# Attention with decay and two MLPs: the softmax's reciprocal sums move from p to x, and p is split in two instructions per head

## The chip, the cores and the metric

The kernel runs on one core of a Trainium2 chip. The core has five engines that run side by side, each through its own list of instructions in order: TensorE (PE, matrix products; its weight loads are the rows PEld), VectorE (DVE), ScalarE (ACT), GpSimd (POOL) and SyncE (SP, which here issues the transfers). They wait for each other by semaphores. The metric is the time of one execution in microseconds, lower is better.

## The reference

```python
scores = q @ k.T / sqrt(64);  decay = cum[:, None] - cum[None, :]      # cum: running sum of log f
scores = where(causal, scores + decay, -1e9) - max
attn = exp(scores);  attn = attn / (sum(attn) + 1e-9)                  # per row (query)
x = (attn @ v)                 # 4 batches x 8 heads, 576 queries, head size 64
x = x.transpose(0, 2, 1, 3).reshape(2304, 512)
h = x @ w_in                   # 512 -> 2048
y = (max(h, 0) + alpha * min(h, 0)) @ w_out
out = ((y @ w_a) * (y @ w_b)) @ w_o          # 512 -> 1536 -> 512
```

## The kernel before

**Attention.** The 32 heads are worked in slots, `attention()`: slot u holds the softmax of head u, the transposition of p of head u-1 and the product of p with v of head u-2 (`lag` 2). What a slot does and in which order is written out as a list of short names, one list for even and one for odd slots: `T` makes the operands of the next head, `s0` to `s3` are scores and softmax of 128 query rows each, `R` those of the last 64 rows of two heads together (a row block `r` for a pair of heads), `ri` and `rr` the reciprocals of the row sums, `h0`..`h4` and `l0`..`l4` the handling of p, `p0` and `p1` the products with v for query columns 0 to 255 and 256 to 575, `M` a place where MLP work is let in. A scheduler of the framework then settles each engine's own order from this program.

**p in two ways.** Heads 0 to 9 ("native") keep p in f32: POOL multiplies each of the four row blocks by its reciprocal sum (`p_hi`, line 393), TensorE transposes it in 128x128 pieces (line 415), and DVE or ACT copy it out of PSUM. Heads 10 to 31 split p into two f16 parts: POOL writes the high part of p times the reciprocal (`p_hi`, line 406), DVE the rest (`p_lo`, line 486), four instructions of each per head, one per row block of 128, 256, 384 and 512 columns, and one of each per pair for `r` (640 columns). A transfer (DMA transpose, line 493) turns row blocks 0 and 1 together (`PT_lo`), 2 and 3 together (`PT_hi`) and `r` (`PT_r`). The f16 tiles `p16` have one buffer each, so the next head's high part waits for the transfer of the last.

**x.** `pv` leaves two halves in PSUM: ACT copies one (line 541), DVE adds the other (line 542). After the second head of a pair ACT rounds x to `xh` (line 204) and POOL subtracts to `xl` (line 548), once per half of the columns. x holds one pair of heads as 128 partitions (2 heads x 64) by 576 queries. Native heads do the same from one PSUM bank (lines 470, 471). After the last head of a batch both parts go to DRAM (line 557).

**Around it.** While the native heads run, 14 weight blocks of the first MLP are loaded and split by ACT, DVE and POOL (`weight`, lines 120 to 130). From slot 10 on, TensorE fills up with the first MLP (`mlp1a`; DVE line 636, POOL line 638), in a quota per slot. After the last slot the attention's buffers are closed, the rest of the first MLP, further weights (line 120 again) and the second MLP follow; there the instructions are the same before and after the change.

Of the kernel before, what the change touches and what calls it, by code (L numbers as in the profile page):

```python
# [35 lines left out]

REBIAS = 2.0 ** -112
_P = dict(
    even="ri T h3 h2 h0 s2 vs M h1 Q s0 M l2 s3 M s1 l1 M l0 l3 p0 p1 V po M W".split(),
    odd="ri h3 h2 h0 R rr vs h1 M Q l2 T l3 s2 M h4 s3 l1 M M s1 l0 s0 p0 p1 V W po l4 M".split(),  # L40
    split=0,
    lag=2,
    eng={'U': 'pool', 'xl': 'pool', 'h0': 'pool', 'h1': 'pool', 'nq': 'act', 'x': 'dve'},
    psm=3,
    first=10,
    rates=[0, 1, 1, 1, 0.8, 1.15, 1.15, 0.95],
# [5 lines left out]
    eng0={'h3': 'pool', 'U': 'pool', 'h1': 'pool', 'e0': 'act', 'e2': 'act', 'e3': 'dve', 'e4': 'dve'},
    even0=['ri', 's3', 'T', 'p0', 'h2', 'h3', 's2', 'vs', 'h1', 's0', 'Q', 'M', 'M', 'M', 'M', 'l1', 'l2', 'h0', 's1', 'l0', 'l3', 'p1', 'V', 'po', 'W', 'M'],
    odd0=['ri', 'h3', 'h2', 'h0', 'R', 'h1', 'rr', 'M', 'Q', 'l2', 'T', 'l3', 'M', 's3', 'h4', 's2', 'l1', 'l0', 'M', 'M', 's1', 's0', 'p0', 'vs', 'p1', 'V', 'W', 'po', 'l4', 'M'],
# [19 lines left out]
def decay_attention_then_two_mlps(ctx, tc, q, k, v, f, w_in, w_out, alpha, w_a, w_b, w_o, out):  # L74
# [135 lines left out]
    def attention_setup():  # L210
        a = lpool(right, "att1", 1, "right")
        ap_["a"] = a
        maskz = a.tile([128, ST + 128 + S - HB], BF16, name="maskz")
# [10 lines left out]
        ap_["mask_r"] = rest

        for i in range(2):
            z = ST + SR * (1 - i)
            t1 = a.tile([128, SP], F32R, tag=f"T1_{i}", name=f"T1_{i}")
            u1 = a.tile([128, S], F32R, tag=f"U1_{i}", name=f"U1_{i}")
            tu2 = a.tile([128, 2 * SP], F32R, tag=f"TU2_{i}", name=f"TU2_{i}")  # L230
            dve.memset(f32(t1)[:, z:z + SR], 0.0)
            dve.memset(f32(tu2)[0:68, z:z + SR], 0.0)
            TU[i] = t1, tu2[:, :SP], u1, tu2[:, SP:SP + S], f32(tu2)
            ap_["s", i] = a.tile([128, 1280], F32, tag=f"s_{i}", name=f"s_{i}")
            for nm in ("nm", "sm", "ri"):
# [244 lines left out]

    def p_lo(n, i):
        if n < NATIVE:
            return p_whole(n, i)
        t, s, ri = p16.pop((n, i))
        g, o = GROUP[i]
        eng(f"l{i}", "dve").scalar_tensor_tensor(t[:, 1::2, :], s, ri, t[:, 0::2, :], op0=ALU.mult, op1=ALU.subtract)
        whole, done_ = p16[n, g]
        done_.append(i)
        if g == "r" or len(done_) == 2:
            PT[n, g] = ap_["a2"].tile(  # L490
                [128, GSIZE[g], 128], F16, tag=f"PT_{g}", name=f"PT_{n}_{g}", bufs=2 if g == "r" else LAG,
            )
            sp.dma_start_transpose(out=PT[n, g], in_=whole.rearrange("p t n -> p (t n)"))
            del p16[n, g]

    def pv(u, c):

# [35 lines left out]
        x32 = xs[g, c]
        x = x32[p0:p0 + 64]
        if eng("x", "dve") is pool:
            y = ap_["a"].tile([128, 256 + SR], F32, tag="y", name=f"y_{u}_{c}")[p0:p0 + 64, :w]
            act.activation(x, ps_o[p0:p0 + 64, :w], AF.Copy, scale=1.0 / PSCALE)
            act.activation(y, ps_o[o0:o0 + 64, :w], AF.Copy, scale=1.0 / PSCALE)
            pool.tensor_tensor(x, x, y, op=ALU.add)
        else:  # L540
            act.activation(x, ps_o[o0:o0 + 64, :w], AF.Copy, scale=1.0 / PSCALE)
            dve.scalar_tensor_tensor(x, ps_o[p0:p0 + 64, :w], 1.0 / PSCALE, x, op0=ALU.mult, op1=ALU.add)
        if j == 0:
            return
        x_tiles(b)
        xh, xl = (x_[:, hp, h0:h0 + w] for x_ in X[b])
        dup(eng("xh", "act"), xh, x32)
        eng("xl", "pool").tensor_tensor(xl, x32, f32(xh), op=ALU.subtract)
# [364 lines left out]
```

## Time and profile before

| what | value |
|---|---|
| median of 3 runs | 1132.21 us (1131.31 to 1134.94) |
| profiled execution | 1132.38 us, span 1130.6 us, mean granted TensorE clock 0.988 |
| native heads with weights | about 20 to 118 us |
| split heads with the first MLP | about 118 to 380 us |
| rest of the first MLP with new weights | about 380 to 440 us |
| from there on TensorE is busy all the time, but for a stretch at 600 to 660 us | to the end |

The span runs from the first to the last instruction. Busy times of engines overlap; a matmul's row lasts longer than the distance to the next one's start, since they are pipelined.

### The profile page before, as it was taken

What the parts mean: (1) busy time and instruction counts of PE and PEld (TensorE: products, weight loads), DVE (VectorE), ACT (ScalarE), POOL (GpSimd) and SP (SyncE); (2) the same over time, 40 slices, a digit from 0 to 9 for tenths busy, and PEclk for the clock granted to TensorE, in tenths of its full rate; (3) what the DMA queues carried; (4) which work ended last, traced back from release to release, by engine and by line L of the source; (5) the groups of instructions that cost most, each with busy time, mean ns of one, the idle gap of its engine ahead of it and who ended that gap; (6) DMA issues with size and microseconds to landing.
All of it is one profiled execution on the core that took longest, in us unless ns stands there. A gap on an engine that the chain in (4) does not pass through costs nothing.

```text
span 1130.6 us, 18926 instructions
## 1 busy us (share of the span) xinstructions
PE 1074.1 (95%) x6663; PEld 1006.2 (89%) x6663; DVE 572.1 (51%) x1360; ACT 525.0 (46%) x1407; POOL 489.4 (43%) x627
## 2 busy tenths in 40 slices
PE   5989999999999988999998899999999999999998
PEld 3768988888888988999998899999999999999997
DVE  5787979888888386787777645200000000000001
ACT  5776776777677465555665544221121111211211
POOL 5554757667576354555566554211111111111111
PEclk9999999999999999999999999999999999999999
DMA  4646366776864774777788883020020200200000
GB/s 108 160 130 182 76 142 121 191 139 122 203 136 87 198 229 126 251 259 254 244 267 271 276 294 115 17 84 1 1 84 1 66 19 1 84 1 1 28 1 28
DMA packets 210772, 141.24 MB, mean 125 GB/s; under 512 B 138421, under 2 KB 196789, under 8 KB 210677
## 3 DMA queue, kind: packets, MB, share of 16 engines
q1 hardware_dynamic: 210676, 140.03, 44.4%
q8 instruction: 52, 0.85, 0.3%
q14 instruction: 44, 0.35, 0.1%
HBM read 88.30 MB, written 33.65 MB: 108 GB/s over the span
## 4 chain that ended last, share of the span: by engine, by line
PE 62%; DVE 16%; DMA 7%; ACT 6%; issue 4%; POOL 4%; SPq 1%; POOLq 0%; ACTq 0%; DVEq 0%
PE a L643 4%; PE a L641 4%; PE a L642 4%; PE b L643 4%; PE b L641 4%; PE b L642 4%; PE o L641 4%; PE o L643 4%; PE o L642 4%; PE hb L641 3%; PE hb L642 3%; PE hb L643 3%; PE ya L641 3%; PE ya L642 3%; PE ya L643 3%
## 5 line engine op out<-in xcount | busy, mean ns | idle before, releaser
L876 DVE TENSOR_TENSOR as<-b,as 128x384 f32<-128x384 f32 x72 | 40.2, 558 | 380.0 <-PE b L643 379.2
L878 POOL TENSOR_TENSOR gg<-as,gg 128x384 fp32r<-128x384 f32 x72 | 73.1, 1016 | 346.3 <-ACT gg L877 346.3
L875 ACT COPY as<-a 128x384 f32<-128x384 f32 x72 | 34.6, 481 | 182.7 <-PE a L643 182.7
L877 ACT CAST gg<-as 128x384 fp32r<-128x384 f32 x72 | 37.1, 515 | 142.3 <-DVE as L876 142.2
L636 DVE SCALAR_TENSOR_TENSOR lt<-lu,nal,lt 128x288 f32<-128x288 f32 (+1 forms) x110 | 79.5, 722 | 45.7 <-ACT lt L635 45.2
L643 PE MATMUL a<-yh,w_a 128*128 128x384 f32 x288 | 97.3, 338 | 0.0
L641 PE MATMUL a<-yh,w_a 128*128 128x384 f32 x288 | 97.1, 337 | 0.0
L643 PE MATMUL b<-yh,w_b 128*128 128x384 f32 x288 | 97.1, 337 | 0.0
L642 PE MATMUL a<-yl,w_a 128*128 128x384 f32 x288 | 97.1, 337 | 0.0
L642 PE MATMUL b<-yl,w_b 128*128 128x384 f32 x288 | 97.1, 337 | 0.0
L641 PE MATMUL b<-yh,w_b 128*128 128x384 f32 x288 | 97.1, 337 | 0.0
L641 PE MATMUL o<-w_o,gg 128*128 128x512 f32 x216 | 84.5, 391 | 0.0
L642 PE MATMUL o<-w_o,gg 128*128 128x512 f32 x216 | 84.4, 391 | 0.0
L352 ACT ACTIVATE s<-s,nm 128x512 f32<-128x512 f32 (+3 forms) x128 | 71.7, 562 | 23.7 <-DVE nm L351 22.8
L643 PE MATMUL o<-w_o,gg 128*128 128x512 f32 x216 | 81.4, 391 | 0.0
L642 PE MATMUL ya<-gb,w_out 128*128 128x384 f32 x216 | 72.8, 337 | 0.0
L642 PE MATMUL y<-g,w_out 128*128 128x288 f32 x224 | 68.2, 308 | 4.8 <-POOL g L638 4.7
L643 PE MATMUL ya<-gb,w_out 128*128 128x384 f32 x216 | 72.6, 336 | 0.0
L641 PE MATMUL h<-xh,w_in 128*128 128x288 f32 x224 | 67.5, 304 | 3.4 <-ACT lt L635 2.0
L638 POOL TENSOR_TENSOR gb<-lt,gb 128x384 fp32r<-128x384 f32 x54 | 56.4, 1045 | 30.9 <-ACT gb L637 28.6
L641 PE MATMUL y<-g,w_out 128*128 128x288 f32 x224 | 66.4, 308 | 2.2 <-ACT g L637 2.2
L642 PE MATMUL h<-xl,w_in 128*128 128x288 f32 x224 | 66.9, 300 | 0.0
(185 smaller groups left out, 3230.0 us busy)
## 6 DMA issues: line engine op xcount, KB each, us to landing
yl<-ya_d SPq DMA_DIRECT2D x48, 192.0 KB
wr_in<-in_moe_w_in SPq DMA_DIRECT2D x32, 256.0 KB
wr_out<-in_moe_w_out SPq DMA_DIRECT2D x32, 256.0 KB
wr_a<-in_moe_w_a SPq DMA_DIRECT2D x24, 256.0 KB
wr_b<-in_moe_w_b SPq DMA_DIRECT2D x24, 256.0 KB
wr_o<-in_moe_w_out SPq DMA_DIRECT2D x24, 256.0 KB
qkn<-in_q SPq DMA_DIRECT2D x64, 72.0 KB
qkn<-in_k SPq DMA_DIRECT2D x64, 72.0 KB
```

The lines of the kernel that those rows point to most:

```text
L352: act.activation(s, s, AF.Exp, bias=nm, scale=-1.0, accum_out=sm)
L636: dve.scalar_tensor_tensor(t, u, nal[:, fi:fi + 1], t, op0=ALU.mult, op1=ALU.add)
L638: pool.tensor_tensor(gl, t, f32(gh), op=ALU.subtract)
L641: pe.matmul(o, lh, rh, start=start, stop=False)
L642: pe.matmul(o, lh, rl, start=False, stop=False)
L643: pe.matmul(o, ll, rh, start=False, stop=stop)
L875: act.copy(asb[:, :n], aps[:, :n])
L876: dve.tensor_tensor(asb[:, :n], bps[:, :n], asb[:, :n], op=ALU.mult)
L877: ap_["last"] = act.copy(g[:, 0, :n], asb[:, :n]).ins
L878: pool.tensor_tensor(g[:, 1, :n], asb[:, :n], f32(g[:, 0, :n]), op=ALU.subtract)
```

## The change

p stays unnormalised. Its two f16 parts are made by two instructions per head on POOL and two on DVE: one over row blocks 0 and 1 together (384 columns, `h0`, `l0`), one over 2 and 3 (896 columns, `h1`, `l1`), times the constant 2^15 in place of the reciprocal; the tile `s` is laid out anew so that these are contiguous. Native heads 0 to 9 lose their four multiplications on POOL. Row block `r` is still normalised as before. The reciprocal of a head's row sums is now written spread over 64 columns (128x4x64), and for each pair of heads TensorE multiplies the four 128x128 pieces with the identity (`rl`, `rinv_rows`), so that the reciprocals stand along the columns as x does; ACT copies the result into `rrow`. x is multiplied with `rrow`: for split heads by POOL, once per pair over 576 columns (`xr`), for native heads by DVE out of PSUM. `xh` and `xl` are made once per pair over all 576 columns. The lists of the slots are written anew.

```diff
-    even="ri T h3 h2 h0 s2 vs M h1 Q s0 M l2 s3 M s1 l1 M l0 l3 p0 p1 V po M W".split(),
-    odd="ri h3 h2 h0 R rr vs h1 M Q l2 T l3 s2 M h4 s3 l1 M M s1 l0 s0 p0 p1 V W po l4 M".split(),
+    even="T h1 h0 ri s2 vs M Q s0 l1 M s3 l0 M s1 M p0 p1 V po M W".split(),
+    odd="rl h1 h0 ri R rr vs M Q l1 T s2 M h4 s3 l0 M M s1 s0 p0 p1 V W po l4 M".split(),
...
+        ap_["rrow"] = a.tile([128, S], F32, name="rrow")
+        pool.memset(ap_["rrow"][:, ST:], 1.0 / PSCALE)
...
+    def rinv(sm, ri, scale):
+        dve.tensor_scalar(sm, sm, 1e-9, scale, op0=ALU.add, op1=ALU.mult)
+        dve.reciprocal(ri, sm.unsqueeze(2).broadcast_to([128, 4, D]) if len(ri.shape) == 3 else sm)
...
+    def rinv_rows(g):
+
+        o = bank(f"rrow_{g}")
+        ri = RI.pop(g)
+        for i in range(4):
+            w = ri[:, i].rearrange("p j d -> p (j d)")
+            pe.matmul(o[:, 128 * i:128 * i + 128], w, ap_["ident"], start=True, stop=True)
+        act.copy(ap_["rrow"][:, 0:ST], o)
...
-            e.tensor_scalar(t[:, 0::2, :], s, ri, 1.0, op0=ALU.mult, op1=ALU.mult)
-        p16[n, i] = t, s, ri
+        g, s, scale = p_parts(n, r)
+        t = p16[n, r] = ap_["a"].tile([128, GSIZE[g], 128], F16, tag=f"p16_{g}", name=f"p16_{n}_{g}")
+        eng(f"h{r}", "pool").tensor_scalar(t[:, 0::2], s, scale, 1.0, op0=ALU.mult, op1=ALU.mult)
...
-        xh, xl = (x_[:, hp, 256 * c:256 * c + w] for x_ in X[b])
-        act.activation(xh, ps_o[:, :w], AF.Copy, scale=1.0 / PSCALE)
-        dve.scalar_tensor_tensor(xl, ps_o[:, :w], 1.0 / PSCALE, f32(xh), op0=ALU.mult, op1=ALU.subtract)
+        cs = slice(256 * c, 256 * c + w)
+        dve.tensor_tensor(x_pair(g)[:, cs], ps_o[:, :w], ap_["rrow"][:, cs], op=ALU.mult)
+        if c == 1:
+            x_out(g)
...
+        x = xs.pop(g)
+        dup(eng("xh", "act"), xh, x)
+        eng("xl", "pool").tensor_tensor(xl, x, f32(xh), op=ALU.subtract)
...
-            act.activation(x, ps_o[o0:o0 + 64, :w], AF.Copy, scale=1.0 / PSCALE)
-            dve.scalar_tensor_tensor(x, ps_o[p0:p0 + 64, :w], 1.0 / PSCALE, x, op0=ALU.mult, op1=ALU.add)
...
+        act.copy(x, ps_o[o0:o0 + 64, :w])
+        dve.tensor_tensor(x, ps_o[p0:p0 + 64, :w], x, op=ALU.add)
+        if j == 1 and c == 1:
+            eng("xr", "pool").tensor_tensor(xs[g], xs[g], ap_["rrow"], op=ALU.mult)
+            x_out(g)
```

On DVE, where head 21's p is split, before (`sm` row sums, `ri` reciprocals, `x_9` x of pair 9, `p_21_hi` and `p_21_lo` the f16 tiles of head 21, `s_159` its p, the rows L351, L319 and L321 the next head's softmax and operands):

```order
L542 SCALAR_TENSOR_TENSOR x_9_0_3197<-pv_0_3365,x_9_0_3197 64x256
L374 TENSOR_SCALAR sm_161<-sm_161 128x4
L375 RECIPROCAL ri_162<-sm_161 128x4
L542 SCALAR_TENSOR_TENSOR x_9_1_3228<-pv_1_3376,x_9_1_3228 64x320
L486 SCALAR_TENSOR_TENSOR p_21_hi<-s_159,ri_162,p_21_hi 128x4x128
L486 SCALAR_TENSOR_TENSOR p_21_hi<-s_159,ri_162,p_21_hi 128x3x128
L351 ISA s_150,nm_151<-sc_2_3461,maskz 128x384
L351 ISA nm_151 128x1
L319 TENSOR_TENSOR TU_1_156<-tqk_0_3433,U_1_155 64x288
L321 TENSOR_TENSOR T_1_154<-tqk_0_3433,T_1_154 64x288
L486 SCALAR_TENSOR_TENSOR p_21_lo<-s_159,ri_162,p_21_lo 128x128
L486 SCALAR_TENSOR_TENSOR p_21_lo<-s_159,ri_162,p_21_lo 128x2x128
```

The same place now:

```order
L513 SCALAR_TENSOR_TENSOR p_21_hi<-s_158,p_21_hi 128x7x128
L376 TENSOR_SCALAR sm_160<-sm_160 128x4
L556 TENSOR_TENSOR x_9_3178<-pv_0_3348,x_9_3178 64x256
L513 SCALAR_TENSOR_TENSOR p_21_lo<-s_158,p_21_lo 128x3x128
L377 RECIPROCAL ri_3236<-sm_160 128x4x64
L556 TENSOR_TENSOR x_9_3178<-pv_1_3357,x_9_3178 64x320
L353 ISA s_150,nm_151<-sc_2_3442,maskz 128x384
L353 ISA nm_151 128x1
```

The split no longer stands behind the reciprocal, four instructions have become two, and the reciprocal (now 128x4x64) stands behind them.

On POOL, at the end of the attention, before (`x_14`, `x_15` the last two pairs, `g` the MLP):

```order
L548 TENSOR_TENSOR xl_4475<-x_14_0_4991,xh_4474 128x256
L548 TENSOR_TENSOR xl_4475<-x_14_1_5022,xh_4474 128x320
L638 TENSOR_TENSOR g_288_4868<-lt_5209,g_288_4868 128x288
L548 TENSOR_TENSOR xl_4475<-x_15_0_5274,xh_4474 128x256
L548 TENSOR_TENSOR xl_4475<-x_15_1_5305,xh_4474 128x320
L638 TENSOR_TENSOR g_0_5442<-lt_5456,g_0_5442 128x288
```

And now:

```order
L658 TENSOR_TENSOR g_288_4838<-lt_5176,g_288_4838 128x288
L558 TENSOR_TENSOR x_14_4957<-x_14_4957,rrow 128x576
L496 TENSOR_TENSOR xl_4480<-x_14_4957,xh_4479 128x576
L558 TENSOR_TENSOR x_15_5237<-x_15_5237,rrow 128x576
L496 TENSOR_TENSOR xl_4480<-x_15_5237,xh_4479 128x576
L658 TENSOR_TENSOR g_0_5409<-lt_5423,g_0_5409 128x288
```

The multiplication with `rrow` stands ahead of each subtraction, and both span all 576 columns.

On TensorE, between the product of p and v of one slot and the next scores of block `r` (`scr`), before (`y` is the first MLP):

```order
L641 MATMUL y_0_2_3242<-g_0_2699,w_out_969 128x288
L642 MATMUL y_0_2_3242<-g_0_2699,w_out_969 128x288
L643 MATMUL y_0_2_3242<-g_0_2699,w_out_969 128x288
L338 MATMUL scr_0_3253<-U_0_146,T_0_145 128x288
L339 MATMUL scr_0_3253<-TU_0_147 128x288
L338 MATMUL scr_0_3253<-U_1_155,T_1_154 128x288
L339 MATMUL scr_0_3253<-TU_1_156 128x288
```

And now, with the four products that turn pair 8's reciprocals:

```order
L661 MATMUL y_0_2_3222<-g_0_2687,w_out_966 128x288
L662 MATMUL y_0_2_3222<-g_0_2687,w_out_966 128x288
L663 MATMUL y_0_2_3222<-g_0_2687,w_out_966 128x288
L394 MATMUL rrow_3226<-ident,ri_2876 128x128 x4
L340 MATMUL scr_0_3239<-U_0_146,T_0_145 128x288
L341 MATMUL scr_0_3239<-TU_0_147 128x288
L340 MATMUL scr_0_3239<-U_1_154,T_1_153 128x288
L341 MATMUL scr_0_3239<-TU_1_155 128x288
```

The four products stand at the head of an odd slot, among MLP work, one pair after another.

## Rows read from the trace of the kernel before

**Rows 1.** Busy time by stretch: us, then each engine's busy us (instructions), clock, DMA.

```profile
core 0: us, PE busy (x) PEld busy (x) DVE busy (x) ACT busy (x) POOL busy (x), PEclk, DMA share, GB/s
...
20.00:118.00 98.00, 89.59 (x527) 71.61 (x526) 75.01 (x248) 73.44 (x221) 50.93 (x79) 0.97 0.56 152
118.00:380.00 262.00, 242.71 (x2098) 226.88 (x2098) 221.09 (x576) 184.03 (x548) 172.04 (x244) 0.99 0.65 134
380.00:440.00 60.00, 53.66 (x360) 51.24 (x359) 38.16 (x75) 33.67 (x93) 31.01 (x36) 0.94 0.70 226
...
660.00:1130.60 470.60, 466.08 (x2459) 438.95 (x2457) 68.03 (x130) 99.29 (x212) 96.60 (x100) 1.00 0.13 44
```

**Rows 2.** Chain that ended last, by line: 118 to 380 us, its longest pieces.

```profile
by line: issue 11.0%; DVE p_hi L486 9.3%; DMA PT_hi<-p_hi 8.0%; DVE s L351 5.6%; DVE p_lo L486 5.5%; DVE T L321 5.2%; DVE TU L319 5.1%; POOL p_hi L406 4.1%; ACT s L352 3.4%; DVE lt L636 3.3%; PE y L642 2.6%; PE y L643 2.4%; POOL g L638 2.2%
...
209.92 8.73 DMA PT_hi<-p_hi
```

**Rows 3.** Waits, 118 to 380 us: engine line <- releaser: us, times, longest.

```profile
ACT s L352 <- DVE nm L351: 22.3, 26, 3.6
...
POOL p_hi L406 <- DVE ri L375: 10.0, 8, 2.9
```

**Rows 4.** DVE by shape, 118 to 380 us: count | busy us, mean ns | idle before.

```profile
L486 DVE SCALAR_TENSOR_TENSOR p_hi<-s,ri,p_hi 128x512 f16<-128x512 f32 x22 | 23.3, 1059 | 6.3 <-POOL p_hi L406 6.2
...
L486 DVE SCALAR_TENSOR_TENSOR p_hi<-s,ri,p_hi 128x384 f16<-128x384 f32 x22 | 17.0, 774 | 0.2
L486 DVE SCALAR_TENSOR_TENSOR p_lo<-s,ri,p_lo 128x256 f16<-128x256 f32 x22 | 15.4, 698 | 0.1
...
L486 DVE SCALAR_TENSOR_TENSOR p_lo<-s,ri,p_lo 128x128 f16<-128x128 f32 x22 | 14.2, 647 | 0.5
...
L486 DVE SCALAR_TENSOR_TENSOR p_r<-sr,rir,p_r 128x640 f16<-128x640 f32 x11 | 12.1, 1102 | 5.5 <-POOL p_r L406 5.4
...
L374 DVE TENSOR_SCALAR sm<-sm 128x4 f32<-128x4 f32 x22 | 4.8, 219 | 8.5 <-ACT s L352 8.1
L375 DVE RECIPROCAL ri<-sm 128x4 f32<-128x4 f32 x22 | 3.9, 177 | 0.7
...
L375 DVE RECIPROCAL rir<-smr 128x1 f32<-128x1 f32 x11 | 1.7, 159 | 0.1
...
L374 DVE TENSOR_SCALAR smr<-smr 128x1 f32<-128x1 f32 x11 | 1.7, 151 | 0.5 <-ACT sr L371 0.3
```

**Rows 5.** POOL by shape, 118 to 380 us.

```profile
L406 POOL TENSOR_SCALAR p_hi<-s,ri 128x512 f16<-128x512 f32 x22 | 16.2, 737 | 27.2 <-DVE ri L375 10.0 <-DMA PT_hi<-p_hi 5.5 <-ACT x L541 4.1
L406 POOL TENSOR_SCALAR p_lo<-s,ri 128x128 f16<-128x128 f32 x22 | 14.5, 661 | 5.6 <-DVE ri L375 5.6
L406 POOL TENSOR_SCALAR p_lo<-s,ri 128x256 f16<-128x256 f32 x22 | 14.0, 637 | 0.0
L406 POOL TENSOR_SCALAR p_hi<-s,ri 128x384 f16<-128x384 f32 x22 | 13.1, 594 | 0.0
...
L548 POOL TENSOR_TENSOR xl<-x,xh 128x320 fp32r<-128x320 f32 x10 | 9.2, 924 | 0.2
L548 POOL TENSOR_TENSOR xl<-x,xh 128x256 fp32r<-128x256 f32 x10 | 8.4, 837 | 5.4 <-ACT xh L204 5.3
```

**Rows 6.** TensorE in order of time, native: start, us, what, count.

```profile
43.37 0.52 PE L415 MATMUL tp<-ident,s 128*128 128x128 f32 x3
43.73 0.60 PE L335 MATMUL sc<-N 128*128 128x256 f32 x2
```

**Rows 7.** ACT by shape, 118 to 380 us.

```profile
L204 ACT CAST xh<-x 128x320 fp32r<-128x320 f32 x10 | 4.6, 461 | 1.8 <-DVE x L542 1.5
L204 ACT CAST xh<-x 128x256 fp32r<-128x256 f32 x11 | 4.5, 405 | 1.5 <-DVE x L542 1.5
```

**Rows 8.** Native, 20 to 118 us: chain that ended last, by line.

```profile
by line: DMA wr_out<-in_moe_w_out 15.5%; DMA wr_in<-in_moe_w_in 13.4%; ACT s L352 9.0%; ACT N L204 8.8%; issue 6.4%; ACT wx_in L124 4.1%; PE pvw L464 4.0%; DVE wx_out L127 3.7%; DVE wx_out L128 3.1%; ACT wx_out L124 3.1%; DVE s L351 2.5%; D
```

**Rows 9.** What the native transposes (line 415) waited for: us, times.

```profile
  POOL s L393: 4.5, 4
```

**Rows 10.** POOL at the end of the attention, in order of time.

```profile
381.55 0.88 POOL L548 TENSOR_TENSOR xl<-x,xh 128x320 fp32r<-128x320 f32 x1 [0.75 <-ACT xh L204]
```

**Rows 11.** SP's transfers behind it, in order of time.

```profile
382.45 0.56 SPq L557 DMA_DIRECT2D xl_d<-xl  x1
...
387.32 2.13 SPq L120 DMA_DIRECT2D wr_in<-in_moe_w_in  x2
```

More of the change, by code (lines that the diff above doesn't have):

```diff
@@ L51 @@
     es=10,
[L52 to L54 removed]
+    eng0={'U': 'pool', 'e0': 'act', 'e2': 'act', 'e3': 'dve', 'e4': 'dve'},
+    even0="l3 s3 T l2 ri p0 s2 vs l1 s0 Q l0 s1 p1 V po W".split(),
+    odd0="l3 R l2 rl ri rr Q T s3 l1 l0 s2 s1 h4 s0 p0 vs p1 V W po l4".split(),
 )
@@ L234, in attention_setup @@
             ap_["s", i] = a.tile([128, 1280], F32, tag=f"s_{i}", name=f"s_{i}")
-            for nm in ("nm", "sm", "ri"):
+            for nm in ("nm", "sm"):
                 ap_[nm, i] = a.tile([128, 4], F32, tag=f"{nm}_{i}", name=f"{nm}_{i}")
@@ L371, in softmax_rest, with rinv_pair @@
         act.activation(s[:, :S], s[:, :S], AF.Exp, bias=nm[:, 0:1], scale=-1.0, accum_out=sm[:, 0:1])
-    def rinv(sm, ri):
-        dve.tensor_scalar(sm, sm, 1e-9, 1.0 / PSCALE, op0=ALU.add, op1=ALU.mult)
-        dve.reciprocal(ri, sm)
+    def rinv(sm, ri, scale):
+        dve.tensor_scalar(sm, sm, 1e-9, scale, op0=ALU.add, op1=ALU.mult)
+        dve.reciprocal(ri, sm.unsqueeze(2).broadcast_to([128, 4, D]) if len(ri.shape) == 3 else sm)
+    RI = {}
+    def rinv_pair(n):
+        g, j = divmod(n, 2)
+        if g not in RI:
+            RI[g] = ap_["a"].tile([128, 4, 2, D], F32, tag="ri", name=f"ri_{g}")
+        return RI[g][:, :, j]
+    def rinv_rows(g):
[5 more added lines that the diff above has]
+        act.copy(ap_["rrow"][:, 0:ST], o)
     PT = {}
@@ L466, in pv_whole, with x_pair, x_out @@
             return
+        cs = slice(256 * c, 256 * c + w)
+        dve.tensor_tensor(x_pair(g)[:, cs], ps_o[:, :w], ap_["rrow"][:, cs], op=ALU.mult)
+        if c == 1:
+            x_out(g)
+    def x_pair(g):
+        if g not in xs:
+            xs[g] = ap_["a"].tile([128, S], F32, tag="x32", name=f"x32_{g}")
+        return xs[g]
+    def x_out(g):
         b, hp = divmod(g, NP)
         x_tiles(b)
-        xh, xl = (x_[:, hp, 256 * c:256 * c + w] for x_ in X[b])
-        act.activation(xh, ps_o[:, :w], AF.Copy, scale=1.0 / PSCALE)
-        dve.scalar_tensor_tensor(xl, ps_o[:, :w], 1.0 / PSCALE, f32(xh), op0=ALU.mult, op1=ALU.subtract)
+        xh, xl = (x_[:, hp] for x_ in X[b])
+        x = xs.pop(g)
+        dup(eng("xh", "act"), xh, x)
+        eng("xl", "pool").tensor_tensor(xl, x, f32(xh), op=ALU.subtract)
     def x_tiles(b):
@@ L479, in x_tiles, with p_lo @@
             )
-    def p_lo(n, i):
+    def p_lo(n, r):
         if n < NATIVE:
[L483 to L494, printed above, removed]
+            if r == 4:
+                p_whole(n, 4)
+            return
+        t = p16.pop((n, r))
+        g, s, scale = p_parts(n, r)
+        eng(f"l{r}", "dve").scalar_tensor_tensor(t[:, 1::2], s, scale, t[:, 0::2], op0=ALU.mult, op1=ALU.subtract)
+        PT[n, g] = ap_["a2"].tile(
+            [128, GSIZE[g], 128], F16, tag=f"PT_{g}", name=f"PT_{n}_{g}", bufs=2 if g == "r" else LAG,
+        )
+        sp.dma_start_transpose(out=PT[n, g], in_=t.rearrange("p t n -> p (t n)"))
     def pv(u, c):
@@ L528, in pv @@
                 passes(ps_o[:, 256:w], t, ptr[:, 2 * t, qs], ptr[:, 2 * t + 1, qs], t == 0, t == NQ - 1)
-        b, hp = divmod(g, NP)
-        if (g, c) not in xs:
-            xs[g, c] = ap_["a"].tile([128, w], F32, tag=f"x32_{c}", name=f"x32_{g}_{c}")
         p0, o0 = 64 * j, 64 * (1 - j)
[L533 to L540, printed above, removed]
-            act.activation(x, ps_o[o0:o0 + 64, :w], AF.Copy, scale=1.0 / PSCALE)
-            dve.scalar_tensor_tensor(x, ps_o[p0:p0 + 64, :w], 1.0 / PSCALE, x, op0=ALU.mult, op1=ALU.add)
[L543 to L548, printed above, removed]
+        cs = slice(h0, h0 + w)
+        x = x_pair(g)[p0:p0 + 64, cs]
+        act.copy(x, ps_o[o0:o0 + 64, :w])
[3 more added lines that the diff above has]
+            x_out(g)
     xs = {}
@@ L592, in attention @@
                     if cur(u - 1):
-                        rinv(ap_["sm", (u - 1) % 2], ap_["ri", (u - 1) % 2])
+                        sm = ap_["sm", (u - 1) % 2]
+                        rinv(sm, rinv_pair(u - 1), 1.0 if u - 1 < NATIVE else PSCALE)
+                elif op == "rl":
+                    if u > 1 and cur(u - 2):
+                        rinv_rows(u // 2 - 1)
                 elif op in ("h4", "l4"):
@@ L599, in attention @@
                     if cur(u - 1):
-                        (p_hi if a == "h" else p_lo)(u - 1, int(i))
+                        if u - 1 >= NATIVE:
+                            (p_hi if a == "h" else p_lo)(u - 1, int(i))
+                        elif a == "l":
+                            late = u >= _P.get("es", 0)
+                            for i in ((1, 2, 3) if i == "1" else (0,)) if late else (int(i),):
+                                p_whole(u - 1, i)
                 elif op == "R":
```

35 lines of the change are left out of this document (12 added, 23 removed).

## The prediction, made before the changed kernel ran

> **What bounds the kernel now.** I read busy time by stretch first [rows 1]. From 660 us to the end TensorE is busy 466.1 of 470.6 us, and nothing there is changed; that part can only begin earlier or later. Between 118 and 380 us, where the split heads run under the first MLP, no engine is full: TensorE 242.7 of 262.0 us (19.3 idle), DVE 221.1 (84%), ACT 184.0, POOL 172.0. Between 20 and 118 us, with the native heads, TensorE is idle for 8.4 of 98 us and DVE busy for 75.0 (77%). So the change pays, or costs, by when the attention ends.
>
> Next the chain of waits in 118 to 380 us [rows 2]. The reader is to see that no line has much: DVE's split of p has 9.3 + 5.5 = 14.8%, the transfers that turn PT_hi 8.0%, POOL's high part 4.1%, DVE's other work most of what follows. The waits say the same from the other side: ACT's exponentials wait 22.3 us for DVE's row minima, and POOL waits 10.0 us in the high part for the reciprocals [rows 3]. DVE is the engine that others wait for, and the change takes work from it.
>
> **The change part by part.**
>
> DVE, the low part. Before, per head, 1059 + 774 + 698 + 647 ns = 3.18 us [rows 4]. Now one instruction of 384 columns, 0.77 us by its row, and one of 896, which the trace does not have. From 384 to 640 columns (774 to 1102 ns) it is 1.28 ns a column, so 896 takes 1102 + 256 x 1.28 = 1430 ns. The new sum is 2.20 us, 0.97 less a head, 21.4 us over 22 heads. Bounds: by the flattest step in these rows (128 to 256 columns, 51 ns) 896 takes 1.20 us and 26.4 us are saved; by the steepest (384 to 512, 285 ns) 1.67 us and 16.1. I take the middle one, since its rows lie nearest.
>
> These rows are long for their columns and uneven, because POOL works on the same rows at the same time. The Trainium skill ("SBUF — State Buffer", section "SBUF: two separate sides") says that DVE with two SBUF inputs and GpSimd share a port pair as a lock, which one of them holds for a whole instruction. By that rule the long instruction could be held up for the whole of POOL's 384-column one (0.59 us [rows 5]); if it came to the steep bound by that, the saving would be 16.1 us instead of 21.4 and the forecast 1125 us. The rows of before do not show which of the two holds for one long instruction.
>
> DVE, the reciprocal. 128x4 takes 177 ns, 128x1 159 [rows 4]; now it writes 128x256. At the 1.28 ns a column of DVE's split, 252 more cost 0.32 us a head, 7.1 us over 22 heads and 3.2 over the 10 native ones. Bounds: nothing, if small sizes are flat, and 6 ns a column (18 ns for 3 columns), 1.5 us a head. I take 1.28, because the multiplication ahead of it rises from 151 to 219 ns over the same step from one to four columns: a step between tiny sizes is no rate. DVE's addition to x keeps its shape. DVE's net is 21.4 - 7.1 = 14.3 us; DVE is busy 84% of the stretch, so I count 84% as time: **-12.0 us**.
>
> POOL. The high part took 737 + 661 + 637 + 594 = 2.63 us a head [rows 5]; now 594 ns and, at 1.12 ns a column (384 to 512), 737 + 384 x 1.12 = 1.17 us, together 1.76. That saves 0.87 us a head, 19.1 us in all. New is the multiplication of x: 256 to 320 columns cost 1.36 ns each, so 576 take 1.27 us; two such instructions replace 837 + 924 ns, 0.78 us more a pair, 8.6 us. POOL's high part had 4.1% of the chain, 10.7 of its 57.8 busy us, a fifth; a fifth of 19.1 is 3.5. The added 8.6 us lie under POOL's own idle third; I put 0.5 on the path. **-3.0 us**; between -6 (the wait for the reciprocal, which the high part no longer has, counts too) and 0.
>
> TensorE. Four products of 128x128 a pair. Three transposes of that shape occupy it from 43.37 to 43.73 us [rows 6], 0.12 us each; so 0.48 us a pair, 5.3 us over 11 pairs. There are 19.3 idle us in the stretch to take it; between 0 and 5.3 I take half, **+2.6 us**. It waits for a reciprocal that was issued one slot earlier; were it late, the next block of scores and all MLP products would stand behind it.
>
> ACT copies 128x512 per pair. At the 0.875 ns a column of its rounding of x (405 to 461 ns [rows 7]) that is 0.63 us, and one rounding of 576 columns, 0.69, replaces 0.87. That is 0.45 a pair, 4.9 us in all, hidden in ACT's 78 idle us, which are mostly waits for DVE; without that cover it would cost 4.9.
>
> Native heads. The chain there goes through weight transfers, 29%, then ACT [rows 8]; POOL's multiplication is not in it. What goes are the 4.5 us that transposes waited for it [rows 9]; what comes are 3.2 us of reciprocals on DVE. The products (5 x 0.48) lie in TensorE's 8.4 idle us. **-1.3 us**, between -5 and +5, since the slots' lists change as well.
>
> End of the attention. POOL's last xl ends at 382.43 [rows 10], x goes out at 382.45, and SP's first new weight transfer stands behind that at 387.32 [rows 11]. Now a multiplication (1.27), a longer rounding (+0.22) and a longer subtraction (1.27 for 0.88) stand there: **+1.9 us**, all on the path, as SP's list is in order.
>
> Sum: -12.0 - 3.0 + 2.6 - 1.3 + 1.9 = -11.8. The profiled execution took 1132.4 us (the median of the runs is 0.2 lower), which gives **1121 us**.
>
> **The rivals.**
>
> (a) POOL gives it back: about 1131. In each odd slot the multiplication and the subtraction of x hold POOL for 2.5 us, with ACT's rounding between; behind them stand the MLP's `g`, the splitting of v and the next operands, and TensorE waits for `g`. For it: the order has the two nearly back to back in several slots. Against it: POOL is busy only 66%, and the high part gives back more (19.1 us) than x takes (8.6). If every pair loses 0.9 us there, 10 of the 11.8 us are gone. Then the change does nothing that is measured.
>
> (b) More than the load: about 1108. The split no longer waits for the reciprocal, and PT_hi's transfer starts earlier in its slot, so that the next head's high part, which needs the same f16 buffer, finds it free. The chain has 8.0% (21 us) of PT_hi's transfers; with half of it gone and DVE's 14.3 us counted in full the sum is -14.3 - 10.5 - 3.0 + 2.6 - 1.3 + 1.9 = -24.6. Against it: the transfers stay as many and as large, one took 8.73 us, and TensorE has only 19.3 idle us.
>
> (c) Slower: about 1151. The reciprocal over 256 columns costs 6 ns a column, as the rows for one and four columns would have it. Then it takes 1.69 us a head; DVE's net in the split heads is 22 x (1.51 - 0.97) = +11.9 us, 10.0 at 84%; in the native ones 15.1, 11.6 at 77%, less the 4.5; with the other terms 10.0 + 7.1 - 3.0 + 2.6 + 1.9 = +18.6. It decides from 3.9 ns a column on, where 252 columns eat the 0.97 us. Against it: the multiplication's own step above. The Trainium skill ("VectorE: DVE Perf Modes", section "Walkthrough: the 8-slice pipeline in each mode", on the hardware budget) says that the reciprocal runs as an iterative division with a repeat count of 8. If that meant eight times 1.28 ns a column, an estimate from that page and the rows, the reciprocal would take some 2.8 us and the kernel end near 1180; the four-column row (18 ns for 3 columns, not 31) does not bear that out.
>
> **How the numbers follow.** The forecast (1109 to 1128) gets 0.61, (a) 0.16, (b) 0.12, (c) 0.11. What a measurement can tell from no change is 0.3%, 1128.8 to 1135.6 us. Forecast and (b) lie below it, with a little of (a): faster 0.74; most of (a) and a little of (c), where the reciprocal is half as dear: same 0.16; slower 0.10. For the range, the sum with the good bounds (DVE 26.4 saved, reciprocal flat: 26.4 x 0.84 = -22.2, TensorE 0, the rest as above) is -24.6, 1108, and with the bad ones (16.1 - 7.1 at 84% = -7.6, POOL 0, TensorE 5.3, native +3, end 1.9) +2.6, 1135. I take 1105 to 1133, which holds the forecast, (a) and most of (b).
>
> **What would show it.** Right: DVE's split near 2.2 us a head and DVE busy below 80% in the stretch of split heads; the last xl some 12 us earlier; from there to the end the same length, but for some 2 us. The reciprocal's row decides on (c): 0.5 us or over 1.2. For (a) POOL's waits grow on ACT's rounding, and TensorE's on `g`; for (b) PT_hi leaves the chain. The prediction is wrong if the 896-column instruction takes over 1.7 us, if the reciprocal is dear, or if the native heads, whose lists were also rewritten, end more than 5 us earlier or later than 118 us.

## The result and the profile after

The changed kernel takes 1145.75 us (median of 4 runs, 1141.67 to 1148.85) where the kernel before takes 1132.0 in the same comparison: ratio 1.0114, 95% interval 1.0071 to 1.0157. It is slower by some 13 us; the prediction had it 11 us faster, and even its range ended at 1133. The profiled execution took 1141.67 us (span 1139.9), the fastest of these runs and 4 us under their median; so the views below show some 9 of the 13 us.

Line numbers shift: DVE's split is now L513 (was L486), POOL's L420 (L406), the reciprocal L377 (L375), POOL's `x` times `rrow` L558, `xl` L496, the products L394, ACT's copy of them L395.

Three of the stretches of [rows 1], with the same columns (us, then busy us of PE, PEld, DVE, ACT and POOL, clock, DMA share, GB/s):

```profile
20.00:118.00 98.00, 86.65 (x531) 69.20 (x531) 83.92 (x234) 71.88 (x209) 32.54 (x41) 1.00 0.51 140
118.00:380.00 262.00, 246.84 (x2127) 233.10 (x2126) 235.98 (x541) 185.92 (x552) 170.37 (x201) 0.99 0.64 135
660.00:1139.90 479.90, 475.39 (x2512) 448.26 (x2510) 71.44 (x135) 102.56 (x219) 101.11 (x105) 1.00 0.14 48
```

DVE was to fall from 84% of the split heads' stretch to below 80%; it rose to 90% (235.98 of 262 us), and from 75.0 to 83.9 us among the native heads. POOL's native work did fall (50.9 to 32.5). DVE by shape, 118 to 380 us (count, busy us, mean ns, then the idle time before), to hold against [rows 4]:

```profile
L377 DVE RECIPROCAL ri<-sm 128x256 f32<-128x256 f32 x23 | 40.1, 1742 | 0.1
...
L513 DVE SCALAR_TENSOR_TENSOR p_hi<-s,p_hi 128x896 f16<-128x896 f32 x22 | 26.3, 1196 | 5.4 <-POOL p_hi L420 5.3
...
L513 DVE SCALAR_TENSOR_TENSOR p_lo<-s,p_lo 128x384 f16<-128x384 f32 x22 | 15.4, 701 | 0.5 <-POOL p_lo L420 0.4
...
L376 DVE TENSOR_SCALAR sm<-sm 128x4 f32<-128x4 f32 x22 | 9.7, 440 | 8.3 <-ACT s L354 8.2
...
L377 DVE RECIPROCAL rir<-smr 128x1 f32<-128x1 f32 x11 | 1.8, 161 | 0.3
```

The split itself is better than forecast: 1196 + 701 ns = 1.90 us a head, forecast 2.20, before 3.18. But the reciprocal over 256 columns takes 1742 ns, where 4 columns took 177 and the forecast had some 500; one column (`rir`) takes 161 (159 before). The scaling of the sums ahead of it, unchanged in shape, rose from 219 to 440 ns. The reciprocal is now DVE's costliest group, and the largest entry of the chain that ended last (118 to 380 us), where DVE's split had been the largest of an engine's work [rows 2]:

```profile
by line: DVE ri L377 7.8%; issue 7.6%; DVE lt L656 4.9%; ACT s L354 4.6%; PE y L662 3.5%; PE y L663 3.2%; PE y L661 3.1%; DVE s L353 3.1%; POOL g L658 3.0%; DVE TU L321 2.6%; DVE T L323 2.6%; PE pv L531 2.6%; DVE p_hi L513 2.4%; PE pv L533 
```

POOL by shape in the same stretch, to hold against [rows 5], and ACT's two new groups:

```profile
L420 POOL TENSOR_SCALAR p_hi<-s 128x896 f16<-128x896 f32 x22 | 22.0, 1001 | 8.5 <-ACT s L354 6.3 <-DMA PT_hi<-p_hi 2.2
L420 POOL TENSOR_SCALAR p_lo<-s 128x384 f16<-128x384 f32 x22 | 17.9, 815 | 2.8 <-ACT s L354 2.3 <-DMA PT_lo<-p_lo 0.4
L558 POOL TENSOR_TENSOR x<-x,rrow 128x576 f32<-128x576 f32 x10 | 14.9, 1490 | 6.2 <-DVE x L556 6.0
L496 POOL TENSOR_TENSOR xl<-x,xh 128x576 fp32r<-128x576 f32 x10 | 14.4, 1439 | 1.8 <-ACT xh L204 1.6
```

```profile
L204 ACT CAST xh<-x 128x576 fp32r<-128x576 f32 x10 | 6.7, 674 | 0.7 <-POOL x L558 0.7
L395 ACT COPY rrow<-rrow 128x512 f32<-128x512 f32 x11 | 6.4, 586 | 1.2 <-PE rrow L394 1.1
```

POOL's split takes 1.82 us a head (forecast 1.76), its two instructions on x 1.49 and 1.44 (1.27 each); ACT's 0.67 and 0.59 (0.69 and 0.63). The waits of the stretch, as in [rows 3]: ACT's for DVE's minima fell from 22.3 to 17.7 us, POOL's high part no longer waits for the reciprocals, and POOL waits 15.9 us for v's transfers (1.6 before):

```profile
ACT s L354 <- DVE nm L353: 17.7, 18, 2.8
...
POOL vs L287 <- DMA vs<-in_v: 15.9, 10, 3.4
```

TensorE in order of time, native, with three transposes ahead of a pair's products; then both lines over the whole run:

```profile
40.22 0.49 PE L428 MATMUL tp<-ident,s 128*128 128x128 f32 x3
40.54 1.06 PE L394 MATMUL rrow<-ident,ri 128*128 128x128 f32 x8
41.44 0.82 PE L477 MATMUL pvw<-PT_lo,vs 128*128 128x256 f32 x4
```

```profile
L394 PE MATMUL rrow<-ident,ri 128*128 128x128 f32 x128 | 17.8, 278 | 0.3 <-ACT TU L204 0.3
L428 PE MATMUL tp<-ident,s 128*128 128x128 f32 x100 | 16.1, 275 | 2.7 <-ACT N L204 1.1 <-ACT PT_hi L204 1.1 <-DVE PT_r L206 0.3
```

Four products are written for a pair, and eight records stand there: a product appears as two, a transpose as one (100 for the ten of each native head). The products of this pair occupy TensorE from 40.54 to 41.44, 0.90 us, where the forecast took 0.48 from transposes [rows 6].

The end of the attention, DVE's last x, POOL, and SP, which answers to [rows 10, 11]:

```profile
388.03 0.84 DVE L556 TENSOR_TENSOR x<-pv,x 64x256 f32<-64x256 f32 x2 [1.76 <-ACT x L555]
```

```profile
389.01 1.43 POOL L558 TENSOR_TENSOR x<-x,rrow 128x576 f32<-128x576 f32 x1 [5.35 <-DVE x L556]
391.23 1.43 POOL L496 TENSOR_TENSOR xl<-x,xh 128x576 fp32r<-128x576 f32 x1 [0.79 <-ACT xh L204]
```

```profile
392.69 0.84 SPq L568 DMA_DIRECT2D xl_d<-xl  x1
...
396.51 2.82 SPq L120 DMA_DIRECT2D wr_in<-in_moe_w_in  x2
```

x goes out 3.8 us after DVE's last x (388.87 to 392.69); before it was 1.5 (380.97 to 382.45). Stage by stage, from marks in the trace (the start of DVE's 128x512 row minimum of heads 0, 10 and 31, POOL's last `xl`, the second MLP's first product `hb`, the last instruction), in us:

| | native 0 to 10 | split 10 to 31 | 31 to last xl | to hb | to the end |
|---|---|---|---|---|---|
| before | 103.0 | 241.7 | 22.7 | 53.3 | 694.9 |
| after | 107.8 | 248.0 | 21.5 | 51.7 | 695.6 |

So 4.8 us were lost among the native heads and 6.3 among the split ones; the three stretches behind them are together 2.1 us shorter.

### The profile page after: what moved, and what is told of

Its sections match the earlier page's. It is cut to its first block, busy times and chain, and to the rows that moved or that the text cites. A ratio compares the mean times of both kernels' runs of the same rounds, so it can differ in the third digit from the quotient of the medians.

```text
span 1139.9 us, 19075 instructions
## 1 busy us (share of the span) xinstructions
PE 1082.2 (95%) x6791; PEld 1017.4 (89%) x6791; DVE 596.1 (52%) x1316; ACT 527.2 (46%) x1407; POOL 473.9 (42%) x549
## 4 chain that ended last, share of the span: by engine, by line
PE 65%; DVE 14%; DMA 7%; ACT 6%; issue 4%; POOL 3%; SPq 1%; POOLq 0%; ACTq 0%; DVEq 0%
PE a L663 4%; PE b L663 4%; PE a L662 4%; PE a L661 4%; PE b L662 4%; PE b L661 4%; PE o L661 4%; PE o L663 4%; PE o L662 4%; PE hb L661 3%; PE hb L663 3%; PE hb L662 3%; PE ya L661 3%; PE ya L662 3%; PE ya L663 3%
## 5 line engine op out<-in xcount | busy, mean ns | idle before, releaser
L354 ACT ACTIVATE s<-s,nm 128x512 f32<-128x512 f32 (+3 forms) x128 | 71.4, 560 | 19.9 <-DVE nm L353 19.3
```

The lines of the kernel that those rows point to most:

```text
L354: act.activation(s, s, AF.Exp, bias=nm, scale=-1.0, accum_out=sm)
```

## The experiments

The first theory after the result was that the reciprocal's price alone turned the sign; the rival, that other terms were wrong too. DVE's busy time below is that of the whole profiled execution, from the page's first part; times are medians, and ratios are to the kernel before, run beside them.

**The reciprocal narrow again, spread by a copy on DVE or on ACT.** The edit to the changed kernel (with `act.copy` in the second):

```diff
-        dve.reciprocal(ri, sm.unsqueeze(2).broadcast_to([128, 4, D]) if len(ri.shape) == 3 else sm)
+        if len(ri.shape) == 3:
+            dve.reciprocal(sm, sm)
+            dve.tensor_copy(ri, sm.unsqueeze(2).broadcast_to([128, 4, D]))
+        else:
+            dve.reciprocal(ri, sm)
```

> The changed kernel, but the reciprocal stays at 128x4 (0.18 us) and a DVE copy spreads it to 128x256, which I put at about 0.4 us. Theory 1: the wide reciprocal (1.74 us a head where 0.50 was forecast) is the whole gap between 1121 and the measured 1146; then this run takes about 1121 us, 1115 to 1127. Theory 2: POOL's two 576-column instructions a pair and the new lists cost most of it and DVE's long reciprocal hides in other waits; then it stays at 1135 to 1146 us.

> The same, but ACT spreads the narrow reciprocal (about 0.4 us a head on ACT, nothing on DVE but 0.18 us). Theory 1, with DVE as the engine that the others wait for: as fast as the copy on DVE or up to 5 us faster, 1113 to 1124. Theory 2: no better than 1135.

On DVE: 1146.54 us (1145.54 to 1148.8), ratio 1.0131 [1.0117, 1.0144]. DVE is busy 27.9 us less (568.2 for 596.1), and nothing came of it: 0.8 us slower, within the 7.2 us over which the changed kernel's own runs spread. On ACT: 1138.62 (1137.35 to 1139.35), ratio 1.0059 [1.0046, 1.0072]; 40.4 us less on DVE gave 7.1 us. The theory that the reciprocal is the whole gap fell: without the wide one the kernel is still slower than before. Both runs came out as theory 2 had them, the first 0.5 us above its range.

**The wide reciprocal in the kernel before** (it writes 128x4x64, and the split reads one column):

```diff
-        dve.reciprocal(ri, sm)
+        if len(ri.shape) == 3:
+            dve.reciprocal(ri, sm.unsqueeze(2).broadcast_to([128, 4, D]))
+        else:
+            dve.reciprocal(ri, sm)
...
-            ri = ap_["rir"][:, 0:1] if i == 4 else ap_["ri", n % 2][:, i:i + 1]
+            ri = ap_["rir"][:, 0:1] if i == 4 else ap_["ri", n % 2][:, i, 0:1]
```

> The kernel before with one edit: its reciprocal writes 128x256 (one column of 64 is then used), so the suspected cost stands alone, 1.56 us more a head on DVE, 32 heads, and here ahead of the split of p. Theory 1: 22 x 1.56 at 84% and 10 x 1.56 at 77% are 41 us, so about 1173, at least 1155. Theory 2, the reciprocal hides: under 1142 us.

1140.94 us (1138.09 to 1143.4), ratio 1.0079 [1.0065, 1.0094]. DVE is busy 34.1 us more (606.2 for 572.1); the time rose by 9.0 (from 1131.92 in the runs beside it), inside theory 2's bound, though 9 us are not nothing. Whatever this work of DVE's is worth on the path, it is not 84%.

**Taking the scaling away, then adding its parts one by one.** The base leaves out the reciprocals of the heads, the products, their copy and POOL's multiplication, so its output is unnormalised (a constant stands in `rrow`, by which DVE still multiplies the native heads' x); three kernels put back one part each.

```diff
-                        rinv(sm, rinv_pair(u - 1), 1.0 if u - 1 < NATIVE else PSCALE)
+                        pass
...
-                    if u > 1 and cur(u - 2):
-                        rinv_rows(u // 2 - 1)
+                    pass
...
-            eng("xr", "pool").tensor_tensor(xs[g], xs[g], ap_["rrow"], op=ALU.mult)
```

> The changed kernel without the scaling of x: it leaves out the reciprocals of the heads' sums, the products that turn them, ACT's copy and POOL's multiplication of split pairs (x comes out unnormalised). What is left is the gain of the two-instruction split with the new lists. Theory A (TensorE's added products count almost in full, 0.21 us each as they take two passes, 13.5 us in all, and the reciprocals the rest): about 1120 us, 1113 to 1125. Theory C (the new lists of the slots are themselves worse, above all in the native heads): 1130 or more.

> The kernel without scaling, plus TensorE's four products a pair, fed from a constant tile, and ACT's copy of their result; no reciprocals, no multiplication by POOL. Theory A: 10 to 14 us above the kernel without scaling, as TensorE's work counts almost in full. Theory B (TensorE's idle time takes the products; what hurts is that they wait for late reciprocals): within 3 us of it.

> The version without any scaling of x (1122.09 us) with one thing added: the reciprocal of each head's row sums over 128x4x64 on DVE, 32 of them, whose result nobody reads; p stays unnormalised, so the output is not attention's. DVE gets 32 x about 1.9 us. Theory A (DVE's time is hidden in part, as in the two runs that changed this reciprocal): 7 to 12 us, 1129 to 1134. Theory of rival (c), each of DVE's busy us counted at 84 and 77%: 22 x 1.74 x 0.84 + 10 x 1.74 x 0.77 = 46 us, 1168. If it costs nothing by itself (under 3 us), what it costs in the changed kernel comes from the products that wait for it.

> The version without any scaling of x (1122.09 us) with one thing added: POOL's multiplication of x over 576 columns, once per pair of split heads, by a row of constants; p stays unnormalised. POOL gets 11 x 1.49 = 16.4 us, one of them at the attention's end, where it is all on the path. The forecast's step (hidden but for the last): 1122.1 + 1.5 = 1123.6, from 1122.5 to 1125. Rival (a) (each pair loses 0.9 us on POOL): 1122.1 + 9.9 + 1.5 = 1133.5. With the products at 8.3 us, the rest up to the version with the spread on ACT (1138.6) is 8.2 us; what this run does not take of it belongs to the narrow reciprocals and the spread.

| kernel | us (runs) | ratio, 95% interval | DVE busy | to the base |
|---|---|---|---|---|
| base | 1122.09 (1120.77 to 1122.68) | 0.9909 [0.9892, 0.9926] | 541.2 | |
| + products and copy | 1130.43 (1126.87 to 1133.73) | 0.9979 [0.9964, 0.9995] | 539.5 | +8.3 |
| + wide reciprocal | 1138.55 (1137.53 to 1141.14) | 1.0056 [1.0037, 1.0076] | 594.8 | +16.5 |
| + x times rrow on POOL | 1124.46 (1123.66 to 1126.14) | 0.9933 [0.9911, 0.9955] | 542.2 | +2.4 |

The base is 10.0 us faster than the kernel before: that is all that the two-instruction split brings, with the native multiplications gone and the small reciprocals too, though DVE is busy 30.9 us less. By the marks of the stages the base's native heads take 103.0 us, as before, and its split heads 231.1 for 241.7, so in these two executions the gain lies in the split heads alone. The three parts sum to 27.2 us, and the base with all of them would be 1149.3; the changed kernel is 1145.75. The 3.5 us between are less than the changed kernel's own spread, so the parts add up as far as these runs can tell.

The base and POOL's part came out as expected. The products' 8.3 us lie between their two theories (10 to 14, and under 3), the reciprocal's 16.5 above theory A's 7 to 12 and far below rival (c)'s 46. Part of a difference may be TensorE's clock, which was not the same in the profiled executions (base, then with the reciprocal):

```profile
118.00:380.00 262.00, 249.04 (x2155) 235.92 (x2154) 193.98 (x490) 183.25 (x547) 157.65 (x192) 0.98 0.69 144
118.00:380.00 262.00, 238.91 (x2005) 222.14 (x2005) 233.25 (x535) 177.78 (x531) 158.36 (x192) 0.96 0.66 136
```

The step from 0.98 to 0.96 over 262 us is some 5 of the reciprocal's 16.5 us, an estimate from these two rows; with the products the clock was 1.00, so their 8.3 us are not the clock's.

**Transposes in place of products**, with the wide reciprocal, and with the narrow one that ACT spreads:

```diff
-            pe.matmul(o[:, 128 * i:128 * i + 128], w, ap_["ident"], start=True, stop=True)
+            pe.transpose(o[:, 128 * i:128 * i + 128], w, ap_["ident"])
```

> The changed kernel with the four products turned into four transposes of the same tile (0.11 us each by the rows of the native heads, for two passes of 0.11 us): the same waits, the same bank, half the TensorE time, 6.7 us less in all. Theory A: 5 to 7 us faster than the changed kernel, about 1139. Theory B: no change, 1145.

> Transposes in place of products and the narrow reciprocal spread by ACT. Theory A: 5 to 7 us below the 1138.6 us of the run with ACT's spread, so 1132 to 1134, level with the kernel before. Theory B: 1138.

With the wide reciprocal 1152.1 us (1151.11 to 1154.44), ratio 1.0179 [1.0159, 1.0199]: 6.4 us slower than the changed kernel, against both theories. With the narrow one 1131.32 (1129.53 to 1132.69), ratio 0.9992 [0.9983, 1.0002]: 7.3 us under its counterpart with products, about the 16 x 0.45 us that half of the products' records take (theory A had 5 to 7). The trace of the slower one shows a part of its loss. First DVE, then TensorE, in order of time about a stall at 311 us:

```profile
310.76 1.38 DVE L513 SCALAR_TENSOR_TENSOR p_hi<-s,p_hi 128x896 f16<-128x896 f32 x1
312.07 1.74 DVE L377 RECIPROCAL ri<-sm 128x256 f32<-128x256 f32 x1
313.84 0.49 DVE L556 TENSOR_TENSOR x<-pv,x 64x320 f32<-64x320 f32 x1
```

```profile
308.23 0.27 PE L531 MATMUL pv<-PT_hi,vs 128*128 128x256 f16 x1
308.34 0.27 PE L532 MATMUL pv<-PT_hi,vs 128*128 128x256 f16 x1
...
310.61 0.28 PE L341 MATMUL sc<-TU 68*128 68x128 f32 x1
314.39 0.80 PE L340 MATMUL sc<-U,T 128*128 128x512 f32 x1 [3.50 <-DVE x L556]
...
319.62 0.42 PE L533 MATMUL pv<-PT_hi,vs 128*128 128x256 f16 x1
319.83 0.42 PE L531 MATMUL pv<-PT_hi,vs 128*128 128x256 f16 x1
```

and the windows around it (columns as above), with all of the split stretch:

```profile
310.00:316.00 6.00, 2.50 (x11) 1.85 (x9) 5.85 (x8) 3.20 (x11) 5.23 (x7) 0.71 0.81 159
316.00:322.00 6.00, 4.87 (x32) 3.66 (x30) 4.83 (x15) 3.47 (x11) 3.01 (x4) 0.50 0.81 221
322.00:332.00 10.00, 10.00 (x81) 9.84 (x79) 9.58 (x20) 8.67 (x25) 3.71 (x6) 0.96 1.02 242
118.00:385.00 267.00, 244.22 (x2062) 229.35 (x2060) 237.04 (x536) 184.83 (x551) 164.11 (x200) 0.96 0.63 131
```

The next scores wait for DVE's addition to x (both use the same ring of banks in PSUM, the memory that TensorE writes to), and that addition stands behind 1.38 us of the split and 1.74 us of the reciprocal. TensorE is idle for 3.50 us. The granted clock falls in this stretch and is 0.50, 1.2 of 2.4 GHz, from 316 to 322 us, where products of 256 columns start 0.21 us apart instead of 0.11. In the changed kernel the clock of the same 267 us is higher:

```profile
118.00:385.00 267.00, 250.75 (x2166) 236.87 (x2165) 236.57 (x542) 187.54 (x556) 173.24 (x202) 0.99 0.65 135
```

0.03 of 267 us is 8.0 us (5 to 11, as both shares are rounded), an estimate of the most that the clock can have cost, beside a difference of the two spans of 10.9, of which 6.3 lie between the marks of heads 10 and 31 (254.3 us for 248.0). In DVE's order in the trace the wide reciprocal stands directly ahead of an addition to x in 6 of the 22 split heads in the changed kernel, in 11 in this one: an edit to TensorE's instruction alone changed DVE's planned order too.

**The same, with the transposes asked for later in the odd list** (`h1 h0 ri rl` for `rl h1 h0 ri`), to see whether another order mends it:

> The version with transposes in place of products (1152.10 us) with the reciprocals' transposes asked for four places later in the odd slots' list; same work, another order on every engine. Theory A (that version lost by the order that came out of planning, not by its transposes): it ends 7 us below the changed kernel or near it, 1136 to 1146. Rival (a transpose of the wide reciprocals costs more than a product by some wait of its own): it stays at 1149 to 1155.

1151.65 us (1150.49 to 1155.42), ratio 1.0167 [1.0142, 1.0193]: the rival's number. The planner again put the reciprocal ahead of x in 11 of the 22 split heads, and the clock of 118 to 385 us is 0.96 again. So this run varied less than it was meant to; it doesn't part the transposes from that order. The trace of the first of the two does speak on the rival:

```profile
L394 PE MATMUL rrow<-ident,ri 128*128 128x128 f32 x64 | 10.0, 276 | 0.0
```

TensorE was idle 0.0 us ahead of its 64 transposes, and they occupy it 10.0 us, where the products take 17.8: so no wait of their own shows. The version with the narrow reciprocal fits that: same transposes, clock 1.00 there, 20.8 us less. That the order is the cause is not shown by itself, since no run has the same instructions in another order without the 11 places.

**Native heads as before, split heads with transposes and ACT's spread** (the edit in part; the native lists of slots are those of before):

```diff
+            s = s_view(n, r)
+            ri = ap_["rir"][:, 0:1] if r == 4 else ap_["ri", n % 2][:, r:r + 1]
+            pool.tensor_scalar(s, s, ri, 1.0, op0=ALU.mult, op1=ALU.mult)
...
-        dve.tensor_tensor(x_pair(g)[:, cs], ps_o[:, :w], ap_["rrow"][:, cs], op=ALU.mult)
+        act.activation(xh, ps_o[:, :w], AF.Copy, scale=1.0 / PSCALE)
+        dve.scalar_tensor_tensor(xl, ps_o[:, :w], 1.0 / PSCALE, f32(xh), op0=ALU.mult, op1=ALU.subtract)
```

> Split heads as in the version with transposes and a narrow reciprocal that ACT spreads (1131.32 us); native heads as before the change, p normalised by POOL, with the lists of slots of before. Theory A (the native stage's 5 us, 103.0 to 108.4 us, come from scaling the native heads' x by way of TensorE, DVE and ACT): 5 us come back, 1126 us (1125 to 1128), faster than before the change. Rival (the native stage is bound by the weights that are loaded under it, and what it saves is waited for in the first MLP): 1130 to 1132.

1124.41 us (1122.78 to 1126.16), ratio 0.9931 [0.9906, 0.9955]: faster than both kernels, and a little below theory A's range. By the same marks as above the native heads take 103.6 us again (108.4 without this edit), and the split heads 232.1 (233.0 without it, 241.7 before the change).

```profile
20.00:118.00 98.00, 87.92 (x539) 70.18 (x538) 77.03 (x252) 75.01 (x225) 53.78 (x82) 1.00 0.55 152
118.00:380.00 262.00, 250.64 (x2198) 237.94 (x2197) 201.74 (x531) 193.98 (x576) 169.23 (x201) 0.99 0.67 143
```

DVE is at 77% of the split stretch, which is what the forecast had wanted of the changed kernel.

## Why the prediction was wrong

The sum by its own terms, in us; "measured" is the difference of two kernels above:

| term | forecast | measured |
|---|---|---|
| DVE's low part and POOL's high part (21.4 at 84%, 3.5), native waits (4.5) | -26 | -10.0 (base) |
| wide reciprocal (7.1 at 84%, native 3.2) | +9.2 | +16.5 |
| products | +2.6 | +8.3 |
| POOL on x, and the end | +2.4 | +2.4 |
| rest, less than the runs' spread | | -3.5 |
| sum | -11.8 | +13.7 |

**"DVE is busy 84% of the stretch, so I count 84% as time"** is the step that failed most: the gain was put at 26 us and measured 10.0. Per busy us of DVE the time changed by 10.0 / 30.9 = 0.32 in the base, 16.5 / 53.6 = 0.31 for the reciprocal added to it, 9.0 / 34.1 = 0.26 in the kernel before, 7.1 / 40.4 = 0.18 between the changed kernel and ACT's spread, and 20.8 / 44.0 = 0.47 between the two versions with transposes. None of these is the price of DVE's work alone: the base takes work off POOL too, ACT's spread puts some on ACT, and orders and clocks differ. But all are far under 0.84. A busy share says how full an engine is, not how often the others wait for it. [rows 2] had given less: DVE's split has 14.8% of the chain, 38.8 us, of the 69.9 that its four instructions are busy [rows 4], or 0.55. The forecast had counted POOL's high part in this way, at a fifth, and DVE not. The instructions themselves came out better than forecast (28.2 us saved over 22 heads, for 21.4). And the 4.5 us of native waits brought nothing that shows: the base's native heads, under lists written anew, take as long as before.

**"A step between tiny sizes is no rate"** was wrong: (1742 - 177) / 252 is 6.2 ns a column, and the discarded step from one column to four had shown 18 / 3 = 6.0. The multiplication beside it, from which the forecast argued, is another kind of operation. So rival (c) had the price, and with it the side. Its 1151 us is nearer than the forecast, but by two errors that offset each other: it too counted DVE at 84%, for the loss as for the gain. Nor is the price the whole account: with ACT's spread the kernel is at 1138.6 us, and if the parts add up, 1122.1 + 8.3 + 2.4 leave 5.8 of it to the narrow reciprocals, their spread and the waits for them. The Trainium skill ("VectorE: DVE Perf Modes", section "Walkthrough: the 8-slice pipeline in each mode") calls the reciprocal an iterative division with a repeat count of 8. The direction agrees with the trace; the factor was 6.2 to 1.33 ns a column (1196 ns for 896), 4.7, not 8.

**The products** were priced by transposes; they take 0.81 to 0.91 us a pair where they stand together, for 0.48, and half of that was taken to lie in idle time. The 19.3 idle us of TensorE were no cover; that idle time which others cause need not lie where the products come is an argument, not a measurement. The 8.3 us include ACT's copy and a PSUM bank; that halving TensorE's part, with the same copy and bank, took 7.3 us away speaks for TensorE.

**POOL on x** was right in size (rival (a) fell: 2.4 us, not 9.9 and more); the end, from DVE's last x to x going out, grew by 2.3 us, forecast 1.9. The worry from the Trainium skill ("SBUF — State Buffer", section "SBUF: two separate sides") that one long DVE instruction waits for a whole POOL instruction isn't borne out on average: 1196 ns here and 1344 in the base, not 1670. But single instructions show it, on DVE and then on POOL:

```profile
282.94 1.68 DVE L513 SCALAR_TENSOR_TENSOR p_hi<-s,p_hi 128x896 f16<-128x896 f32 x1 [0.62 <-POOL p_hi L420]
```

```profile
282.88 0.80 POOL L658 TENSOR_TENSOR g<-lt,g 128x288 fp32r<-128x288 f32 x1
283.64 1.35 POOL L420 TENSOR_SCALAR p_lo<-s 128x384 f16<-128x384 f32 x1
```

Here POOL's `g` began first, and DVE's 896 columns took 1.68 us; then POOL's 384 columns began beside DVE and took 1.35. At 161 to 163 us, where the two meet for 0.04 us only, they took 1.09 and 0.51. So a long instruction can cost POOL as well: its 384 columns had a mean of 815 ns, 594 before.

**The native heads** had -1.3, between -5 and +5; they lost 4.8 us (head 10 begins at 123.2 us, for 118), and the last experiment gives such a loss back. **Rival (b)**: PT_hi's 8.0% did leave the top of the chain, and whatever it bought lies within the base's 10.0 us.

**What stays open.** Why DVE's own spread gained nothing for 27.9 us less on DVE: its split stage is 246.4 us for 248.0, but the native one (110.0 for 107.8) and that from head 31 to the last `xl` (25.9 for 21.5) are longer, under an order of its own. And how much of each difference is the edit, how much the order that the planner made of it: an order held fixed under two edits wasn't tried.

## What to carry to other kernels

Price a new operation by its own kind, and take a slope between two small sizes seriously where the operation is one that may be slow for each element. Count an engine's freed time as time only as far as the chain and the waits name it; here, at a busy share of 84%, a busy us was worth 0.18 to 0.47 us. When a change is a gain and several costs tied together, build the gain alone and each cost alone: a version that wins (1124.4 us, with transposes, ACT's spread and the native heads left alone) was hidden in a change that lost.

## What the runs showed of the hardware that was not expected

- A reciprocal on DVE: 1742 ns for 128x256 in f32, 6.2 ns a column, beside 1.33 for a multiply-subtract of 896 columns and 407 ns for ACT's copy of the same 128x256.
- An f32 product of 128x128 stands as two records 0.112 us apart, a transpose as one: 128 records for 64 products.
- About a stall of 3.50 us TensorE's granted clock fell, and it was still 1.2 of 2.4 GHz in the 6 us from 316 to 322, in which products of 256 16-bit columns started 0.21 us apart instead of 0.11. That stall cost more than its length. Less idle time stood ahead of a fall at times: in the changed kernel 1.52 us between 133 and 136 us came before 0.50 from 136 to 139, and 1.79 us between 212 and 215 before a full clock.
- DVE's 896 columns took 1.09 us by themselves and 1.68 where POOL's `g` had begun before them; POOL's 384 columns took 0.51 us by themselves and 1.35 where DVE's had.
